# The last inverse products of a long convolution, split by token tile and moved around its frequency loop

## The chip, the cores and the metric

The kernel runs on one core of one Trainium2 chip. The metric is the device time of one execution in microseconds: before the change the median of three runs is 718.02 us (716.53 to 719.85). All matmuls work on fp32 data, or on fp32 data split into a high and a low part.

## The reference, cut to what matters

One adaLN block over 2048 tokens of 512 channels: a diagonal state-space convolution, added to the input, then a Dense-Mish-Dense MLP with 1792 hidden units, added again.

```python
mod = (silu(c) @ w_mod)                 # six rows of 512: sa, ca, ga, sb, cb, gb
h = layernorm(x) * (1 + ca) + sa
K = einsum("dn,dnl,dn->dl", C, exp(dt*A*l), dt*B).real     # the convolution's kernel
y = irfft(rfft(h padded) * rfft(K padded))[:2048] + h * Dskip
x = x + ga * y
h = layernorm(x) * (1 + cb) + sb
x = x + gb * (mish(h @ w1 + b1) @ w2)
```

## The kernel before, in words

The FFT is a matrix product in two stages, on both sides. The kernel has four parts in time.

**Generation** (to about 247 us). 32 groups of 16 channels go through `s_ang`, `s_sin`, `comb`, `s_kgen`, `s_ks`, `s_skip`, `s_ka` and `s_tm`; the last two apply the first DFT stage to K, and `s_tm` copies each group into its columns of the SBUF tile `gk` (128 x 32 x 512). In the same loop the tokens get their first layer norm and their first DFT stage (`pua`) and go out to the DRAM tensor `ud`. Which call stands in which of the 32 turns is a table (`pe`, `se`, `ve`, `vt`, filled by `at`). The six vectors of the modulation come from `mod_mm` (the first three) and, near the end of the loop, `mod_piece` (tile `pmq`).

**The frequency loop** (to 343.5 us), 16 steps q. A step has three products of four matmuls each: `pub` (second DFT stage of the tokens, from `ur`, which is loaded from `ud`), `pkb` (second stage of K, from `gk`), and `pz`, the first inverse stage of the step before. Between them VectorE makes the complex product Y of `pub` (copied to `f` by ScalarE) and `pkb`: two multiplications of 128x1024 and two sums of 128x512. `pz` has 128 output rows for each of the two frequencies of q; ScalarE copies it to `z`, which goes to the DRAM tensor `zd`. In the loop w1 is loaded too, in eight pieces (`w1s`), each split by a cast on ScalarE (`w1h`) and a subtraction on VectorE (`w1l`).

**Between the loop and the MLP.** Rows 32t to 32t+31 of every `pz` belong to token tile t (512 tokens). `z_load` reads a tile's rows back in another order (`zl`), `inv_a` applies the second inverse stage (`pia`), adds the result to x and takes the statistics, `ln_norm` normalizes (`xn`), and `ln_t` transposes (`pln`), applies the modulation on VectorE (`hf`) and on ScalarE (`hh`, the high part), and subtracts the two for the low part.

**The MLP**, four token tiles of 14 hidden blocks: `mm1` (`pm`, 12 matmuls), Mish on ScalarE, a split into `mah` and `mal`, and, two blocks later (LAG), `mm2` (`po`, 12 matmuls). The later tiles do their `z_load`, `inv_a`, `ln_norm` and `ln_t` inside the tile before. `load_w2` loads w2 in four pieces during the first blocks and splits them (`w2h`, `w2l`).

**What sets the order.** Every instruction goes through helpers, so that nearly all of them have one line in the profile (L147 the matmuls, L119 VectorE and ScalarE); names of tiles tell them apart. Matmuls issued by `mm` keep the order of the program; those of the MLP, issued directly, are ordered by the framework's scheduler. VectorE and ScalarE keep the order of the program where the flags `V.on`, `A.on` are set, which is so only in the generation. Each DMA is issued by the instruction stream of the engine that is named: `nc.sync` is SyncE, which does nothing else; a DMA issued through `A` takes its turn on ScalarE. Tile pools opened on the place of closed ones wait for the users of the old tiles.

Of the kernel before, what the change touches and what calls it, by code (L numbers as in the profile page):

```python
# [36 lines left out]
def _constants():  # L37
# [25 lines left out]
    for d in range(16):  # L63
# [21 lines left out]
def s4_block(ctx, tc, io, out):  # L85
# [532 lines left out]
    for n, k, d in ((0, 4, ve), (1, 7, vt), (2, 10, ve), (3, 12, ve), (4, 15, vt), (5, 17, ve), (6, 20, ve), (7, 23, vt)):  # L618
# [13 lines left out]
    at(se, NG - 1, mod_last)  # L632
    at(se, NG - 6, second_part)
    at(se, NG - 2, ur_load, 0)
    at(se, NG - 1, ur_load, 1)
    at(pe, NG - 1, pub, 0, psum)
    at(se, NG, pub_out, 0)

    for k in range(NG + 1):
        tc.cur_priority = 100000 + 10000 * k  # L640
        for s in [(s_kgen, k - 1), (s_ang, k + 3), (s_ka, k - 3)] + pe.get(k, []):
# [19 lines left out]
    s_skip(NG - 1)  # L661
    for f in s_ka, s_tm:
        f(NG - 2)
    for f in s_ka, s_tm:
        f(NG - 1)
    pub(1, psum)
    pub_out(1)
    V.on = A.on = False
# [42 lines left out]

    def inverse(q):
        p = pair("pz", f"pz{q}", 1)
        mi = MQ["mi", q // 4].rearrange("p (q c) x -> p q c x", c=2)
        for c in range(2):
            for r in range(2):
                mm(p[:, r, :], mi[64 * r:64 * r + 64, q % 4, c, :], Y[q][64 * r:64 * r + 64, c, :],
                         start=(c == 0), stop=(c == 1))
        z = yp.tile([P, 2, D], F32, tag="z", name=f"z{q}")
        A.copy(z, p)  # L720
        nc.sync.dma_start(view(zd, 2 * q * D, [[ZROW, P], [1, 2 * D]]), z.rearrange("p r d -> p (r d)"))

# [29 lines left out]
    def z_load(tt, hv):  # L752
        z = ZL[tt, hv] = mp.tile([P, 2, 2, D], F32, tag="z", name=f"zl{tt}{hv}")
        for g in range(4):
            (A if tt == 0 and g % 2 else nc.sync).dma_start(z[32 * g:32 * g + 32].rearrange("p j t d -> p (j t) d"),
                              view(zd, (8 * (4 * tt + g) + 4 * hv) * ZROW, [[D, 32], [ZROW, 4], [1, D]]))

    def inv_a(tt, hv):
        for j in range(2 * hv, 2 * hv + 2):
            p = bank("pia")  # L760
            for tl in range(2):
                T.matmul(p[64 * tl:64 * tl + 64, :], di, ZL[tt, hv][:, j % 2, tl, :], start=True, stop=True)  # L762
            x = X2[tt][:, j]
            V.tensor_add(x, x, p)
            st = keep.tile([P, 6], F32, tag="bst2", name="bst2", bufs=2)
            V.bn_stats(st, x)
            V.bn_aggr(mv2[:, 4 * tt + j, :], st)
# [22 lines left out]
    def mm1(tt, f):  # L790
# [4 lines left out]
        for k in range(KB):  # L795
            for wi, hi in ((0, 0), (0, 1), (1, 0)):
                T.matmul(p, w1[wi][:, k, fs], hh[:, hi, k, :], start=(n == 0), stop=(n == 3 * KB - 1))  # L797
# [9 lines left out]
    def mm2(tt, f, qs=range(4)):  # L807
# [3 lines left out]
        for q in qs:  # L811
            n = 0
            for ai, wi in ((0, 0), (0, 1), (1, 0)):
                T.matmul(PO[tt][q], a[ai][:, P * q:P * q + P], w2[wi][:, f, :],  # L814
                         start=(f == 0 and n == 0), stop=(f == FB - 1 and n == 2))
# [10 lines left out]
    V.tensor_scalar(modt[:, 1], modt[:, 1], 1.0, None, op0=OP.add)  # L826
# [19 lines left out]
    for n, (tt, f) in enumerate(seq):  # L846
        mm1(tt, f)
        if n < 4:
            load_w2(4 * n)
        if tt + 1 < 4:  # L850
            if f == 4:
# [56 lines left out]
```

## Time and profile before

| | us |
|---|---|
| median of three runs | 718.02 |
| the profiled execution, its own time | 714.55 |
| its span, first to last instruction | 712.8 |
| TensorE busy in the span | 634.3 (89%) |
| VectorE busy | 412.8 (58%) |
| ScalarE busy | 319.9 (45%) |

The profile is of one execution. Times in its rows count from the start of the span. A row of the timeline has start, duration, engine, line, operation, output and inputs, and in brackets the idle time of the engine just before and what ended it; a row of the chain of waits has start and duration of a piece of the chain that ended last. PE is TensorE, DVE is VectorE, ACT is ScalarE; SPq and ACTq are the DMA issues of SyncE and ScalarE. PEclk is the TensorE clock that was granted, as a share of full speed.

### The profile page before, as it was taken

Reading aid. Unit: us, or ns where it says so; the run is one execution under the profiler, and the core shown is the slowest. Engines: PE = TensorE matmul, PEld = TensorE weight load, DVE = VectorE, ACT = ScalarE, POOL = GpSimd, SP = SyncE. Lnnn points to the kernel's source line nnn. Section 1 sums busy time; section 2 is a strip of 40 time slices with the busy share of each in tenths; the row PEclk is TensorE's granted clock in tenths of the full one; section 3 lists DMA queues with packets and bytes.
Section 4 is the critical chain, followed back from the end, with each engine's and each line's share of the span. In section 5 each row is a group of like instructions: output and inputs, shape, how many; then the busy total and the mean of one; then the engine's idle time right before and its main releaser. Section 6 shows DMA issues by size and latency. Waiting matters only on the chain.

```text
span 712.8 us, 11831 instructions
## 1 busy us (share of the span) xinstructions
PE 634.3 (89%) x4848; PEld 432.8 (61%) x4848; DVE 412.8 (58%) x813; ACT 319.9 (45%) x466; POOL 5.0 (1%) x12
## 2 busy tenths in 40 slices
PE   0488899889989979999249999999999999999995
PEld 0356666556656623333028778887788867888884
DVE  8889989997976657876196242342443224441113
ACT  2477798598897644543135212322132211322220
POOL 2000000000000000000000000000000000000000
PEclk9969979879969999999669999999999999999999
DMA  7842213624342479973686140052201400020002
GB/s 194 296 135 66 90 41 111 195 74 151 118 146 93 133 202 316 307 228 131 163 240 139 37 101 0 1 119 59 60 1 29 90 0 1 1 57 4 0 1 59
DMA packets 34315, 74.63 MB, mean 105 GB/s; under 512 B 5419, under 2 KB 9903, under 8 KB 33749
## 3 DMA queue, kind: packets, MB, share of 16 engines
q1 hardware_dynamic: 33380, 72.17, 34.9%
q10 hardware_dynamic: 576, 1.05, 0.7%
q8 instruction: 38, 0.62, 0.4%
q0 software_dynamic: 304, 0.66, 0.4%
q14 instruction: 17, 0.13, 0.1%
HBM read 49.73 MB, written 24.13 MB: 104 GB/s over the span
## 4 chain that ended last, share of the span: by engine, by line
PE 69%; DVE 21%; ACT 4%; DMA 3%; issue 2%; SPq 0%; ACTq 0%; DVEq 0%
PE pm L797 22%; PE po L814 22%; DVE ec L119 8%; PE pub L147 4%; PE pz L147 4%; DVE raw L119 4%; PE pkb L147 4%; PE pang L147 3%; PE pkg L147 2%; PE pka L147 2%; PE pia L762 2%; PE pco L147 2%; DVE x L119 1%; PE pua L147 1%; ACT ec L141 1%
## 5 line engine op out<-in xcount | busy, mean ns | idle before, releaser
L797 PE MATMUL pm<-hh,w1h 128*128 128x512 f32 x448 | 142.5, 398 | 0.6 <-ACT hh L119 0.6
L141 ACT ACTIVATE mh<-pm,b 128x512 f32<-128x512 f32 x56 | 38.5, 688 | 228.2 <-PE pm L797 228.2
L119 DVE TENSOR_TENSOR mal<-mh,mah 128x512 fp32r<-128x512 f32 x56 | 38.7, 691 | 155.3 <-ACT mah L119 155.0
L797 PEld LDWEIGHTS pm<-hh,w1h 128*128 128x128 f32 x448 | 84.8, 189 | 21.6 <-ACT hh L119 1.5
L814 PE MATMUL po<-w2h,mah 128*128 128x512 f32 x224 | 89.4, 399 | 0.0
L797 PE MATMUL pm<-hh,w1l 128*128 128x512 f32 x224 | 88.7, 396 | 0.0
L814 PE MATMUL po<-w2l,mah 128*128 128x512 f32 x224 | 88.6, 395 | 0.0
L814 PE MATMUL po<-w2h,mal 128*128 128x512 f32 x224 | 88.5, 395 | 0.0
L119 DVE TENSOR_TENSOR ec<-ec,co 128x1024 f32<-128x1024 f32 x64 | 75.0, 1204 | 8.4 <-ACT ec L141 8.4
L147 PE MATMUL pang<-ac,s 96*128 96x512 f32 x128 | 53.2, 461 | 25.8 <-DMA s<-pkd 25.8
L147 PEld LDWEIGHTS pkg<-ec 128*32 128x32 f32 x2048 | 35.9, 114 | 29.4 <-issue 15.4
L119 DVE TENSOR_TENSOR y<-pkb,f 128x1024 f32<-128x1024 f32 x32 | 37.7, 1220 | 27.5 <-PE pkb L147 27.5
L814 PEld LDWEIGHTS po<-w2h,mah 128*128 128x128 f32 x224 | 42.1, 188 | 14.6 <-ACT mah L119 4.9
L147 PE MATMUL pkg<-ec 128*32 128x64 f32 x2048 | 42.0, 230 | 7.6 <-DVE ec L119 6.7
L797 PEld LDWEIGHTS pm<-hh,w1l 128*128 128x128 f32 x224 | 42.3, 189 | 10.0
L814 PEld LDWEIGHTS po<-w2h,mal 128*128 128x128 f32 x224 | 42.1, 188 | 10.2
L814 PEld LDWEIGHTS po<-w2l,mah 128*128 128x128 f32 x224 | 42.1, 188 | 9.8
L147 PEld LDWEIGHTS pang<-ac,s 96*128 96x128 f32 x128 | 27.6, 215 | 32.9 <-issue 26.3
L147 PE MATMUL pang<-am,s 96*128 96x512 f32 x128 | 43.5, 425 | 0.0
L147 PE MATMUL pco<-mc,s 64*128 64x512 f32 x64 | 30.4, 624 | 11.2 <-ACT co L141 7.1
L141 ACT ACTIVATE ec<-ec,halfpi 128x1024 f32<-128x1024 f32 x32 | 37.5, 1173 | 0.0
L147 PE MATMUL pka<-bdk,ks 128*64 128x128 f32 x512 | 36.5, 288 | 0.9 <-ACT gk L119 0.9
(97 smaller groups left out, 832.2 us busy)
## 6 DMA issues: line engine op xcount, KB each, us to landing
ud<-u SPq DMA_DIRECT2D x16, 512.0 KB, 3.4
ur<-ud SPq DMA_DIRECT2D x32, 256.0 KB, 4.3
zd<-z SPq DMA_DIRECT2D x16, 512.0 KB, 3.3
zl<-zd SPq DMA_DIRECT2D x28, 256.0 KB, 4.9
x<-in_A_u SPq DMA_DIRECT2D x32, 128.0 KB, 3.0
x<-in_A_u SPq DMA_DIRECT2D x8, 512.0 KB, 6.9
out<-ot SPq DMA_DIRECT2D x32, 128.0 KB, 2.3
w1s<-in_B_w SPq DMA_DIRECT2D x8, 448.0 KB, 6.0
```

The costliest lines, as they stand in the source:

```text
L119: ins = getattr(self.engine, name)(*a, **kw)
L141: follow("act", nc.scalar.activation(out, in_, f, **kw))
L147: follow("pe", T.matmul(out, lhsT, rhs, start=start, stop=stop))
L762: T.matmul(p[64 * tl:64 * tl + 64, :], di, ZL[tt, hv][:, j % 2, tl, :], start=True, stop=True)
L797: T.matmul(p, w1[wi][:, k, fs], hh[:, hi, k, :], start=(n == 0), stop=(n == 3 * KB - 1))
L814: T.matmul(PO[tt][q], a[ai][:, P * q:P * q + P], w2[wi][:, f, :], start=(f == 0 and n == 0), stop=(f == FB - 1 and n == 2))
```

## The change

1. **Steps 8 to 15 split the inverse product.** New functions `first` and `first_out` compute only the 32 output rows of token tile 0, with 32 weight columns a matmul; the four steps of a group go to four column groups of the array, so that one tile `pf` holds four steps. Steps 8 to 11 are done at step 12, steps 12 to 15 at step 15. The full `inverse` of steps 8 and 9 runs at steps 14 and 15; those of steps 10 to 15 (`late`) run after the loop, three before `pia` and three behind it. They compute all 128 rows, and store rows 32 to 127.
2. **The rows of tile 0 have their own DRAM tensors** (`z0d`), and are loaded by `zl_load` in three groups into `gk`; the first two inside the loop. The layout of `di` has a second copy for that order of rows. In steps 0 to 7 `inverse` stores `z` in three DMAs in place of one, and all of these DMAs are issued by ScalarE.
3. **Y overwrites K** in `gk` (`product`), which frees the tiles `y1` and, once `pz` is done, the place for item 2.
4. **`pub` runs two steps ahead** of `pkb`, and `pz` stands behind both; `pub` of step 1 moves into the generation, with the loads of `ur`, `w_mod` and the second pair of DFT matrices moved earlier.
5. **The modulation row is loaded as 8 x 128** (`modr`) and transposed on TensorE, in place of a load of single elements.
6. **Program order** now binds the matmuls of the MLP, too, and VectorE and ScalarE from the end of the loop until the fifth block of the MLP.
7. **The last tile's results** use four buffers in place of two, and half of their stores go through ScalarE's queue.

```diff
+    z0d = {(g, r): dram.tile([32 * n, D], F32, name=f"z0d{g}{r}") for g, n in enumerate((8, 4, 4)) for r in range(2)}
...
-    for k, pieces in (20, range(4)), (22, (4, 5)), (23, (6, 7)), (26, (8, 9)), (29, (10, 11)):
+    for k, pieces in (20, range(4)), (20, (4, 5)), (23, (6, 7)), (25, (8,)), (25, (9,)), (27, (10,)), (27, (11,)):
...
-        at(pe, NG - 5 + k, mod_piece, k)
+        at(pe if k else vt, 26 + k, mod_piece, k)
...
-    at(pe, NG - 1, pub, 0, psum)
-    at(se, NG, pub_out, 0)
+    at(se, 30, load_mq, 1)
+    for q in range(2):
+        at(pe, 29 + q, pub, q, psum)
+        at(se, 30 + q, pub_out, q)
...
     def product(q):
-        if q > 1:
-            ur_load(q)
-            pub(q, psum)
-            pub_out(q)
...
-        y = Y[q] = yp.tile([P, 2, D], F32, tag="y1", name=f"y1_{q}")
+        y = Y[q] = gk[0][:, 2 * q:2 * q + 2, :]
...
-    def inverse(q):
-        p = pair("pz", f"pz{q}", 1)
+    def inverse(q, p, pool, tag):
...
-        nc.sync.dma_start(view(zd, 2 * q * D, [[ZROW, P], [1, 2 * D]]), z.rearrange("p r d -> p (r d)"))
+        if q < 8:
+            for r in range(2):
+                A.dma_start(z0d[0, r][32 * q:32 * q + 32], z[0:32, r])
+        A.dma_start(view(zd, 32 * ZROW + 2 * q * D, [[ZROW, 96], [1, 2 * D]]), z[32:P].rearrange("p r d -> p (r d)"))
+
+    def first(g, qs):
+        if g not in PF:
+            PF[g] = pair("pz", f"pf{g}", 1)
+        for c in range(2):
+            for r in range(2):
+                for q in qs:
+                    mm(PF[g][32 * (q % 4):32 * (q % 4) + 32, r, :], mi(q, c, r, slice(0, 32)),
+                       Y[q][64 * r:64 * r + 64, c, :], start=(c == 0), stop=(c == 1))
+
+    def first_out(g):
+        for r, (copy, queue) in enumerate(((V.tensor_copy, nc.sync), (A.copy, A))):
+            z = yp.tile([P, D], F32, tag="z", name=f"zf{g}{r}")
+            copy(z, PF[g][:, r, :])
+            queue.dma_start(z0d[g - 1, r], z)
...
+    def zl_load(g, r):
+        q, n = ((0, 8), (8, 4), (12, 4))[g]
+        k = 64 * r + 4 * q
+        nc.sync.dma_start(gk[0][k:k + 4 * n, 0:8, :], view(z0d[g, r], 0, [[8 * D, 4 * n], [D, 8], [1, D]]))
+
+    for q in range(NQ):
+        product(q)
...
+        if q + 2 < NQ:
+            pub(q + 2, psum)
+            pub_out(q + 2)
+        if 0 < q <= 8:
+            inverse(q - 1, pair("pz", f"pz{q - 1}", 1).rearrange("p r d -> r p d"), yp, "z")
+        if q in (10, 11):
+            zl_load(0, q - 10)
+        if q == 12:
+            first(2, range(8, 12))
+            first_out(2)
+        if q >= 14:
+            inverse(q - 6, pair("pa", f"pz{q - 6}", 1).rearrange("p r d -> r p d"), io4, "i")
...
+        if q == 15:
+            first(3, range(12, 15))
+            first(3, (15,))
+            first_out(3)
+            for r in range(2):
+                zl_load(2, r)
...
-                T.matmul(p, w1[wi][:, k, fs], hh[:, hi, k, :], start=(n == 0), stop=(n == 3 * KB - 1))
+                mm(p, w1[wi][:, k, fs], hh[:, hi, k, :], start=(n == 0), stop=(n == 3 * KB - 1))
...
-            nc.sync.dma_start(rows(out, tl, 4 * tt + q, 1), o[64 * tl:64 * tl + 64])
+            (A if tt == 3 and tl else nc.sync).dma_start(rows(out, tl, 4 * tt + q, 1), o[64 * tl:64 * tl + 64])
...
+    V.on = A.on = True
+    for q in range(10, 13):
+        late(q)
     for hv in range(2):
-        z_load(0, hv)
-    for hv in range(2):
-        inv_a(0, hv)
-        ln_norm(0, 2 * hv, 2)
+        run(inv_a(0, hv))
+    for q in range(13, 16):
+        late(q)
...
+    for ops in ln_norm(0, 0, 4):
+        run(ops)
     ln_t(0)
```

**TensorE from the last steps of the loop to the first block of the MLP.** A row has line, operation, output, inputs, size and, with x, how many follow one another. Before:

```order
L147 MATMUL pub_3506<-ur_3503,mf_3279 64x512 x4
L147 MATMUL pkb_3513<-gk,mf_3279 64x512 x4
L147 MATMUL pz_3524<-y_14_3489,mi_3281 128x512 x4
L147 MATMUL pz_3536<-y_15_3518,mi_3281 128x512 x4
L762 MATMUL pia<-zl_3559,di 64x512 x4
L762 MATMUL pia<-zl_3564,di 64x512 x4
```

Now:

```order
L150 MATMUL pub_3440<-ur_3412,mf_3350 64x512 x4
L150 MATMUL pf_3447<-gk,mi_3216 32x512 x16
L150 MATMUL pkb_3471<-gk,mf_3350 64x512 x4
L150 MATMUL pub_3481<-ur_3437,mf_3350 64x512 x4
L150 MATMUL pkb_3488<-gk,mf_3350 64x512 x4
L150 MATMUL pz_3498<-gk,mi_3216 128x512 x4
L150 MATMUL pkb_3510<-gk,mf_3350 64x512 x4
L150 MATMUL pz_3520<-gk,mi_3216 128x512 x4
L150 MATMUL pf_3528<-gk,mi_3352 32x512 x16
L895 MATMUL pmt<-ident,modr 128x8
L150 MATMUL pz_3572<-gk,mi_3216 128x512
L150 MATMUL pia<-gk,di 64x512 x8
```

Steps 9 to 13 have no `pz` any more; two groups of 16 short matmuls stand in the loop. Behind the second come the three late inverses of four matmuls each (the row of `pz_3572` is the first of the twelve), then `pia`, then the other three.

**ScalarE at the start of the loop.** Before:

```order
L144 ACT_TABLE_LOAD
L119 CAST w1h<-w1s_3085 128x896
L119 CAST w1h<-w1s_3147 128x896
L119 COPY z_3082<-pz_3077 128x1024
L119 COPY f_3097<-pub_3092 128x1024
L119 COPY z_3115<-pz_3110 128x1024
```

Now:

```order
L147 ACT_TABLE_LOAD
L122 CAST w1h<-w1s_3116 128x896
L122 CAST w1h<-w1s_3180 128x896
L122 COPY f_3084<-pub_3079 128x1024
L122 COPY f_3104<-pub_3099 128x1024
L122 COPY z_3111<-pz_3106 128x1024
L122 DMA z0d_79<-z_3111 32x512
L122 DMA z0d_80<-z_3111 32x512
L122 DMA zd<-z_3111 96x1024
L122 CAST w1h<-w1s_3248 128x896
L122 COPY f_3138<-pub_3133 128x1024
```

Three DMA issues follow each copy `z`. The copies `f` of steps 2 and 3 come before the first `z`, both behind the two first casts, as `z` of step 0 was.

**VectorE, the modulation of token tile 0** (`hh0`; the numbers tell the four pieces apart). Before:

```order
L119 TENSOR_SCALAR hf_3639<-pln_3634,modt_3044 128x512
L119 TENSOR_SCALAR hf_3648<-pln_3643,modt_3044 128x512
L119 TENSOR_TENSOR w2l_3674<-w2s4_3723,w2h_3673 128x512
L119 TENSOR_TENSOR hh0_3633<-hf_3639,hh0_3633 128x512
L119 TENSOR_TENSOR hh0_3633<-hf_3648,hh0_3633 128x512
L119 TENSOR_SCALAR hf_3657<-pln_3652,modt_3044 128x512
L119 TENSOR_SCALAR hf_3666<-pln_3661,modt_3044 128x512
```

Now:

```order
L122 TENSOR_SCALAR hf_3694<-pln_3689,modt_3059 128x512
L122 TENSOR_TENSOR hh0_3688<-hf_3694,hh0_3688 128x512
L122 TENSOR_SCALAR hf_3703<-pln_3698,modt_3059 128x512
L122 TENSOR_TENSOR hh0_3688<-hf_3703,hh0_3688 128x512
L122 TENSOR_SCALAR hf_3712<-pln_3707,modt_3059 128x512
L122 TENSOR_TENSOR hh0_3688<-hf_3712,hh0_3688 128x512
```

The order is now `hf`, low part, `hf`, low part; the splits of w2 stand behind all four pieces.

More of the change, by code (lines that the diff above doesn't have):

```diff
@@ L208, in s4_block @@
     da = conv.tile([P, P], F32, name="da")
-    di = keep.tile([P, 64], F32, name="di")
+    di = keep.tile([P, 2, 64], F32, name="di")
     ident = keep.tile([P, P], F32, name="ident")
@@ L660, in s4_block @@
             step(s_mag, k + 1)
[L661 to L667, printed above, removed]
+    for i in NG - 2, NG - 1:
+        step(s_skip, i)
+        s_ka(i)
+        s_tm(i)
     V.on = A.on = False
@@ L754, in z_load @@
         for g in range(4):
-            (A if tt == 0 and g % 2 else nc.sync).dma_start(z[32 * g:32 * g + 32].rearrange("p j t d -> p (j t) d"),
+            nc.sync.dma_start(z[32 * g:32 * g + 32].rearrange("p j t d -> p (j t) d"),
                               view(zd, (8 * (4 * tt + g) + 4 * hv) * ZROW, [[D, 32], [ZROW, 4], [1, D]]))
     def inv_a(tt, hv):
-        for j in range(2 * hv, 2 * hv + 2):
+        zl = ZL[tt, hv] if tt else gk[0][:, 4 * hv:4 * hv + 4, :].rearrange("p (j t) d -> p j t d", j=2)
+        v = Later()
+        js = range(2 * hv, 2 * hv + 2)
+        for j in js:
             p = bank("pia")
             for tl in range(2):
[L762 to L767, printed above, removed]
+                mm(p[64 * tl:64 * tl + 64, :], di[:, 0 if tt else 1, :], zl[:, j % 2, tl, :])
+            v.tensor_add(X2[tt][:, j], X2[tt][:, j], p)
+        st = [keep.tile([P, 6], F32, tag="bst2", name="bst2", bufs=2) for j in js]
+        for t, j in zip(st, js):
+            v.bn_stats(t, X2[tt][:, j])
+        for t, j in zip(st, js):
+            v.bn_aggr(mv2[:, 4 * tt + j, :], t)
+        return v.ops
     def ln_norm(tt, q0, n):
         i = 4 * tt + q0
-        rsqrt(rst2[:, i:i + n], mv2[:, i:i + n, 1], n, keep, f"rsq{n}")
+        v, w = Later(), Later()
+        rsqrt(rst2[:, i:i + n], mv2[:, i:i + n, 1], n, keep, f"rsq{n}", v)
         for q in range(q0, q0 + n):
             i = 4 * tt + q
-            y = LNX[tt, q] = mp.tile([P, D], F32, tag="xn", name=f"xn{tt}{q}", bufs=4)
-            V.tensor_scalar(y, X2[tt][:, q], mv2[:, i, 0:1], rst2[:, i:i + 1], op0=OP.subtract, op1=OP.mult)
+            y = LNX[tt, q] = mn.tile([P, D], F32, tag="xn", name=f"xn{tt}{q}", bufs=4)
+            w.tensor_scalar(y, X2[tt][:, q], mv2[:, i, 0:1], rst2[:, i:i + 1], op0=OP.subtract, op1=OP.mult)
+        return v.ops, w.ops
     def ln_t(tt):
-        hh = HT[tt] = mp.tile([P, 2, KB, 512], F32R, tag="hh", name=f"hh{tt}")
+        hh = HT[tt] = (mp if tt % 2 else mn).tile([P, 2, KB, 512], F32R, tag="hh", name=f"hh{tt}", bufs=1)
         for b in range(NB):
@@ L813, in mm2 @@
             for ai, wi in ((0, 0), (0, 1), (1, 0)):
-                T.matmul(PO[tt][q], a[ai][:, P * q:P * q + P], w2[wi][:, f, :],
-                         start=(f == 0 and n == 0), stop=(f == FB - 1 and n == 2))
+                mm(PO[tt][q], a[ai][:, P * q:P * q + P], w2[wi][:, f, :],
+                   start=(f == 0 and n == 0), stop=(f == FB - 1 and n == 2))
                 n += 1
@@ L819, in fin_q @@
         x = X2[tt][:, q]
-        o = mp.tile([P, D], F32, tag="ot", name="ot")
+        o = mn.tile([P, D], F32, tag="xn", name="ot", bufs=4) if tt == 3 else mp.tile([P, D], F32, tag="ot", name="ot")
         V.tensor_mul(o, PO[tt][q], gbb)
@@ L823, in fin_q, with late @@
         for tl in range(2):
-            nc.sync.dma_start(rows(out, tl, 4 * tt + q, 1), o[64 * tl:64 * tl + 64])
-    V.tensor_scalar(modt[:, 1], modt[:, 1], 1.0, None, op0=OP.add)
+            (A if tt == 3 and tl else nc.sync).dma_start(rows(out, tl, 4 * tt + q, 1), o[64 * tl:64 * tl + 64])
+    def late(q):
+        inverse(q, [psum.tile([P, 512], F32, tag="po", name=f"pz{q}{r}") for r in range(2)], io4, "i")
+    p = bank("pmt")
+    follow("pe", T.transpose(p[:, 0:8], modr, ident[0:8, 0:8]))
+    V.tensor_copy(modt[:, 0], p[:, 0:4])
+    V.tensor_scalar(modt[:, 1], p[:, 4:8], 1.0, None, op0=OP.add)
     tables("mish")
+    V.on = A.on = True
+    for q in range(10, 13):
+        late(q)
     for hv in range(2):
-        z_load(0, hv)
-    for hv in range(2):
-        inv_a(0, hv)
-        ln_norm(0, 2 * hv, 2)
+        run(inv_a(0, hv))
+    for q in range(13, 16):
+        late(q)
+    left2.close()
+    left.close()
+    mp = ctx.enter_context(tc.tile_pool(name="mp", bufs=2, side="right"))
+    for ops in ln_norm(0, 0, 4):
+        run(ops)
     ln_t(0)
@@ L849, in s4_block @@
             load_w2(4 * n)
+        if n == 4:
+            V.on = A.on = False
         if tt + 1 < 4:
@@ L855, in s4_block @@
             if f in (6, 8):
-                inv_a(tt + 1, f // 2 - 3)
+                run(inv_a(tt + 1, f // 2 - 3))
             if f == 9:
-                ln_norm(tt + 1, 0, 4)
+                for ops in ln_norm(tt + 1, 0, 4):
+                    run(ops)
             if f == 12:
```

76 lines of the change are left out of this document (46 added, 30 removed).

## The prediction

> **What bounds the kernel now.** I read the busy time by stage first, then the chain of waits, then single rows. In the view by stage the columns are the stretch, its length, the busy time of TensorE, its weight loads, VectorE, ScalarE and GpSimd, each with its count of instructions, then the granted clock, the DMA engines' share and GB/s.
>
> ```profile
> 262.00:341.50 79.50, 78.13 (x338) 24.64 (x336) 58.61 (x67) 34.71 (x35) 0.00 (x0) 0.99 0.72 231
> 341.50:357.00 15.50, 4.21 (x14) 1.62 (x16) 0.66 (x2) 1.01 (x1) 0.00 (x0) 0.63 0.76 197
> 357.00:373.00 16.00, 6.73 (x28) 2.86 (x24) 15.24 (x48) 5.05 (x9) 0.00 (x0) 0.71 0.83 242
> 400.00:700.00 300.00, 300.00 (x1310) 235.32 (x1309) 95.83 (x183) 75.94 (x114) 0.00 (x0) 1.00 0.15 32
> ```
>
> TensorE sets the pace of the frequency loop and of the MLP. Between them, for 31.5 us, it is busy for 11. So the MLP can only start earlier, and the loop only lose products. The chain of waits shows the loop's step and what stands between:
>
> ```profile
> 329.12 1.87 PE pub L147 x8
> 330.99 1.72 PE pkb L147 x8
> 332.71 1.92 PE pz L147 x8
> ...
> 341.55 2.00 PE pz L147 x8
> 344.66 2.59 DMA zd<-z
> 347.89 6.44 DMA zl<-zd
> 354.77 1.99 PE pia L762 x4
> 373.14 10.26 PE pm L797 x36
> 383.40 2.79 PE po L814 x12
> ```
>
> A step is 1.87 + 1.72 + 1.92 = 5.5 us. The last product ends at 343.54; the copy, the store to `zd` and the load of `zl` take until 354.77; statistics, norm and transposes until 373.14; and three blocks of `pm` end at 383.40, from where `po` and `pm` alternate without a gap. I compare both kernels at that point, the end of the third `pm`: 383.40 - 343.54 = 39.9 us behind the loop.
>
> **The sum**, against the profiled execution's own 714.55 us (span 712.8; the median of the runs is 3.5 above, and I add the same).
>
> *Into the loop.*
>
> ```profile
> 240.46 1.09 PE L147 MATMUL pka<-bdk,ks 128*64 128x128 f32 x16 [0.85 <-ACT gk L119]
> 250.37 0.58 ACT L119 COPY gk<-pka 128x512 f32<-128x512 f32 x1 [0.49 <-PE pka L147]
> 253.19 3.65 PE L147 MATMUL pkb<-gk,mf 128*64 128x512 f32 x16 [1.16 <-ACT f L119]
> 257.80 0.94 ACT L119 CAST w1h<-w1s 128x896 fp32r<-128x896 f32 x1 [2.41 <-DMA w1s<-in_B_w]
> 259.47 3.02 PE L147 MATMUL pz<-y,mi 64*128 64x512 f32 x8 [2.62 <-DVE y L119]
> 262.42 2.55 PE L147 MATMUL pub<-ur,mf 128*64 128x512 f32 x8
> ```
>
> With two `pub` among the last turns of the generation, the waits of 0.85 and 1.16 go, and one of about 0.6 (the last copy to `gk`, 0.58) comes: 1.4 gained, `pkb` of step 0 at 251.8. Before, 2.62 us passed without a matmul until Y was ready, and the next two groups ran long (3.02 - 1.92 and 2.55 - 1.87, 1.8 together): 4.4. Now two `pub` stand there. But the second needs the tile that ScalarE's copy `f` frees, and that copy is queued behind the two casts, which end at 258.74 with the load; so that `pub` starts at about 259.2, 2 us after `pkb` of step 1 has ended (251.8 + 1.72 + 1.87 + 1.72 = 257.1). I keep 2.4 of the 4.4; the bounds are 0 and 4.4. Sum: 3.8.
>
> *The loop.* Six `pz` leave it: 6 x 1.92 = 11.5. Two groups `pf` come. No row shows 64 rows by 32 columns; the nearest are these:
>
> ```profile
> 241.48 1.06 PE L147 MATMUL pmq<-wm,sc 128*32 128x512 f32 x6
> 332.82 2.36 DVE L119 TENSOR_TENSOR y<-pkb,f 128x1024 f32<-128x1024 f32 x2 [1.82 <-PE pkb L147]
> 335.21 1.30 DVE L119 TENSOR_TENSOR y<-y,y 128x512 f32<-128x512 f32 x2
> ```
>
> `pz` runs its four matmuls two at a time (two row groups) in 1.92, so 0.96 a round; `pmq` runs three in three column groups in 1.06. A `pf` is 16 matmuls on eight different tiles: two rounds, 1.9, if row and column groups add up; four rounds, 3.8, if four run at once. I take 2.0, since `pmq` shows that column groups with different data run together and `pz` the same of row groups. The two cost 4; the bounds are 3.8 and 7.7. In steps 9 to 13 `pkb` and `pub` are 3.6 us, and VectorE's part of a step 3.7 (332.82 to 336.51): there it sets the pace, but over the whole tail TensorE's sum (30.1 us from `pkb` 9 to the end of `pf`) still covers it. The wait for the last Y stays, now ahead of `pf` of step 15. So 11.5 - 4 = 7.5.
>
> [...]
>
> Against it stands ScalarE, which now issues the stores:
>
> ```profile
> 334.71 1.02 ACT L119 COPY z<-pz 128x1024 f32<-128x1024 f32 x1 [2.62 <-PE pz L147]
> 347.50 1.80 ACTq L119 DMA_DIRECT2D zl<-zd  x4
> ```
>
> An issue takes 0.45 us. In the first steps ScalarE has `f` and `z` (1.0 each), three issues (1.35) and a cast or two (0.94 each): 4.3 to 5.3 of 5.5 us, and what waits for a load there (the 2.41 above) now holds the copies and the stores behind it. From below the cost is 0, from above the 2.41 three times, 7.2: I take 2. Loop: 5.5 gained; together with the entry the last `pf` ends at 343.5 - 9.3 = 334.2.
>
> *From the loop to the MLP.* All loads of `zl`, from issue to landing:
>
> ```profile
> DMA to landing us min/median/max: 3.3/5.0/9.9
> ```
>
> A copy of 0.6 to 0.7, a store (2.59 before, for twice the bytes: 2.4), and a load of twice 256 KB in place of 2 MB (the shortest landing, 3.3, plus 0.9 for two issues): 7.4 us to `pia` in place of 11.2. Three late inverses, 5.8 us, fit in, and three more behind `pia`, where VectorE is the chain:
>
> ```profile
> 356.86 0.69 DVE L119 TENSOR_TENSOR x<-x,pia 128x512 f32<-128x512 f32 x1 [14.85 <-PE pia L762]
> 358.31 0.18 DVE L119 BATCH_NORM_AGGREGATE mv<-bst 128x2 f32<-128x6 f32 x1
> 360.16 0.17 DVE L119 TENSOR_SCALAR rsq<-mv 128x2 f32<-128x2 f32 x1
> 361.75 0.16 DVE L119 SCALAR_TENSOR_TENSOR rst<-rsq,rst 128x2 f32<-128x2 f32 x1
> 364.55 0.99 DVE L119 TENSOR_SCALAR xn<-x,mv,rst 128x512 f32<-128x512 f32 x2
> 371.47 1.53 DVE L119 TENSOR_SCALAR hf<-pln,modt 128x512 f32<-128x512 f32 x2
> ```
>
> The first two `pia` 0.95, four sums and four statistics of 0.69, four aggregates of 0.18: 7.2; twelve small operations at 0.2 (nine lie between 360.16 and 361.91), 2.4 where there were 24 (two roots become one); four `xn`, 2.0; transposes and semaphores 0.5. That is 12.1 us from `pia` to the first `hf`, against 371.47 - 354.77 = 16.7.
>
> Then the new order costs. ScalarE's `hh` waits for `hf`, and the low part for `hh`:
>
> ```profile
> 448.66 0.81 DVE L119 TENSOR_SCALAR hf<-pln,modt 128x512 f32<-128x512 f32 x1
> 449.51 0.78 ACT L119 ACTIVATE hh<-pln,modt 128x512 fp32r<-128x512 f32 x1 [0.74 <-DVE hf L119]
> 450.32 0.69 DVE L119 TENSOR_TENSOR hh<-hf,hh 128x512 fp32r<-128x512 f32 x1 [0.25 <-ACT hh L119]
> ```
>
> With `hf` of one piece behind the low part of the piece before, a piece takes 0.85 + 0.81 + 0.69 = 2.35 us, four 9.4, and the first block, bound to its place, ends 0.5 later; two more blocks are 5.6: 15.5, where it was 383.40 - 371.47 = 11.9. Since the first block keeps TensorE busy for a third of that time, the clock counts:
>
> ```profile
> 256.90:259.40 2.50, 0.00 (x0) 0.00 (x0) 2.50 (x4) 0.94 (x1) 0.00 (x0) 1.00 1.08 249
> 259.40:262.40 3.00, 2.93 (x8) 0.83 (x8) 3.00 (x5) 0.00 (x0) 0.00 (x0) 0.65 0.84 186
> 374.00:376.40 2.40, 2.40 (x6) 1.91 (x7) 2.40 (x5) 1.91 (x4) 0.00 (x0) 0.51 0.41 85
> ```
>
> A pause of 2.5 us is followed by 3 us at 0.65; from the first `pm` at 373.14 half the clock lasts to 376.4 at least, 3.3 us. The same here costs half of that, 1.5. Behind the loop: 7.4 + 12.1 + 15.5 + 1.5 = 36.5, against 39.9: 3.4 gained. [...]
>
> w2 is loaded when the last late store has landed:
>
> ```profile
> 358.49 0.40 SPq L840 DMA_DIRECT2D w2s<-in_B_w  x1
> 364.43 2.18 ACT L119 CAST w2h<-w2s 128x512 fp32r<-128x512 f32 x4 [19.80 <-DMA w2s<-in_B_w]
> ```
>
> The last late copy ends some 18.5 us behind `pf`, its store 21, the load (5.9) 27; its casts are due after the first Mish at 31: covered, by 4 us. The 1024-element load of `modt` was off the path, so item 5 is worth nothing.
>
> *The end.*
>
> ```profile
> 705.92 0.69 DVE L119 TENSOR_TENSOR ot<-po,gbb 128x512 f32<-128x512 f32 x1 [1.64 <-DMA out<-ot]
> ```
>
> Four buffers take that wait away: 1.6.
>
> Total: 3.8 + 5.5 + 3.4 + 1.6 = 14.3. Profile 714.55 - 14.3 = 700.2; median 718.0 - 14.3 = **703.7 us**.
>
> **The rivals.**
> *Faster still*: no wait for casts or stores (2), `pub` at the entry not held (2), the clock kept (1.5): 20, so 698. For it, the rows of 262 to 341 show no stall with casts in line; against it, the stores leave SyncE, which had nothing else.
> *ScalarE as the bound of the first steps*: each cast waits for a load, the load for a buffer, and the stores stand behind. Price: the 7.2 above in place of 2, and once the 1.8 of slowed groups that followed a pause before: 7.0, so 711. For it, the DMA share in the entry's rows is 1.08 and 0.84, so that loads that come earlier land later; against it, `f` is now needed two steps after it is made.
> *w2 late*: its load landed after 5.9 us before; the longest `zl` took 9.9, and the last late store could be slower by as much. With 8 us in all, 4 beyond the cover are lost: 708. With 15, 715: no measurable change.
> *Slower*: the `pf` matmuls run one after another, 16 x 0.96 = 15.4 each. Then the two cost 31 in place of 4, and the time is 703.7 + 27 = 731; it decides from 2.0 + 14.3/2 = 9.2 us a group on. Against it: three `pmq` in 1.06.
>
> **Chances.** The forecast (700 to 707) 0.50, faster still 0.22, ScalarE 0.17, w2 late 0.07 (a third of it within the noise), slower 0.04. What a measurement can tell from no change is about 0.5%, 3.6 us: so faster 0.91 (the upper end of ScalarE's case falls within), same 0.05, slower 0.04. Range 694 to 712, with the first three cases in it; the forecast's own is 700 to 707.
>
> **What would show it.** `pf` groups of about 2 us; `pkb` of step 0 at 251.8; steps 2 to 8 at 5.5 us, and where longer, `pub` or `pz` waiting for ScalarE; the last `pf` ending near 334 and `pia` 7.4 behind; four pieces of `hf` 2.35 apart; the third `pm` done 36.5 behind `pf`; TensorE without a gap from there. The forecast is wrong if `pf` takes over 4 us, if the loop's steps grow, or if `po` waits for `w2h`.

## The result, and the profile after

The changed kernel takes **713.0 us** (median of 7, 710.1 to 714.9) where the kernel before takes 717.8 (median of 7, 716.5 to 719.9): a ratio of 0.9932, 95% interval 0.9913 to 0.995, so it is 0.7% or 4.8 us faster. Forecast were 703.7 us, in a range of 694 to 712. The direction is right, the gain a third of the forecast, and the time lies 1 us above the range.

The profiled execution of the changed kernel took 713.02 us (span 711.2). That of before took 714.55, 3.2 less than its median, so the two traces differ by 1.5 us only. They are compared by the lengths of the stages, each between two rows that both traces have: the first `pkb`; the end of the last `pz` (before) or `pf` (after); the first `hf` of the first token tile; the first `po`; the start of the last `pm`; the end of the last `ot`.

| stage, us | before | forecast | after |
|---|---|---|---|
| start of the first `pkb` | 253.2 | 251.8 | 252.8 |
| loop: to the end of the last `pz` or `pf` | 90.4 | 82.4 | 89.1 |
| to the first `hf` | 27.9 | 19.5 | 20.7 |
| to the first `po` | 11.8 | 17.0 | 17.5 |
| to the last `pm` | 313.6 | 313.6 | 317.2 |
| to the end of the last `ot` | 11.9 | 10.3 | 10.3 |

(Forecast column: 334.2 - 251.8; 7.4 + 12.1; 15.5 + 1.5; no gap; 11.9 - 1.6.) Two stages are off: the loop by 6.7 us and the MLP by 3.6. The one behind the loop came nearly as worked out, its loss at `hf` included.

**The loop.** The view by stage, first after, then before (stretch, length, busy time of TensorE, its weight loads, VectorE, ScalarE and GpSimd with their counts, granted clock, DMA share, GB/s):

```profile
262.00:282.00 20.00, 19.62 (x86) 5.91 (x82) 14.85 (x18) 8.42 (x10) 0.00 (x0) 1.00 0.97 293
282.00:302.00 20.00, 15.63 (x61) 4.73 (x63) 13.96 (x15) 8.53 (x10) 0.00 (x0) 0.91 0.84 256
```

```profile
282.00:302.00 20.00, 20.00 (x88) 6.27 (x86) 15.94 (x18) 9.82 (x11) 0.00 (x0) 1.00 1.00 318
```

In 282 to 302 TensorE, busy throughout before, stood still for 4.4 us and lost more to the clock (granted 0.91). The timeline of TensorE of the changed kernel shows where (in brackets the idle time and what ended it):

```profile
279.68 1.94 PE L150 MATMUL pkb<-gk,mf 128*64 128x512 f32 x8
282.88 1.94 PE L150 MATMUL pub<-ur,mf 128*64 128x512 f32 x8 [1.26 <-ACT f L122]
285.79 1.99 PE L150 MATMUL pz<-gk,mi 64*128 64x512 f32 x8 [0.97 <-ACT z L122]
287.70 1.94 PE L150 MATMUL pkb<-gk,mf 128*64 128x512 f32 x8
...
293.88 3.18 PE L150 MATMUL pz<-gk,mi 64*128 64x512 f32 x8 [2.52 <-ACT z L122]
296.99 2.39 PE L150 MATMUL pkb<-gk,mf 128*64 128x512 f32 x8
...
323.55 1.94 PE L150 MATMUL pub<-ur,mf 128*64 128x512 f32 x8 [2.29 <-DMA ur<-ud]
325.42 1.95 PE L150 MATMUL pf<-gk,mi 64*32 64x512 f32 x32
...
338.57 3.31 PE L150 MATMUL pf<-gk,mi 64*32 64x512 f32 x32
...
351.14 3.65 PE L150 MATMUL pia<-gk,di 128*64 128x512 f32 x16 [2.28 <-DMA zd<-z]
...
366.49 0.50 PE L150 MATMUL pm<-hh,w1h 128*128 128x512 f32 x1 [0.80 <-ACT hh L122]
...
467.31 0.50 PE L150 MATMUL po<-w2h,mah 128*128 128x512 f32 x1 [0.78 <-DVE ot L122]
```

`pkb` starts 8.0 us apart, then 9.3, where 5.5 were forecast; the waits are for ScalarE's copies `f` and `z`, and after the longest the next two groups run at a lower clock (3.18 us for 1.99, granted 0.61 from 293.8 to 297.1; then 2.39 for 1.94, granted 0.80 from 297.0 to 299.4). ScalarE's timeline of that stretch:

```profile
280.98 0.94 ACT L122 CAST w1h<-w1s 128x896 fp32r<-128x896 f32 x1 [4.46 <-DMA w1s<-in_B_w]
281.82 1.01 ACT L122 COPY f<-pub 128x1024 f32<-128x1024 f32 x1
283.89 0.94 ACT L122 CAST w1h<-w1s 128x896 fp32r<-128x896 f32 x1 [1.05 <-DMA w1s<-in_B_w]
284.73 1.00 ACT L122 COPY z<-pz 128x1024 f32<-128x1024 f32 x1
...
289.99 0.94 ACT L122 CAST w1h<-w1s 128x896 fp32r<-128x896 f32 x1 [0.67 <-DMA w1s<-in_B_w]
291.98 0.94 ACT L122 CAST w1h<-w1s 128x896 fp32r<-128x896 f32 x1 [1.05 <-DMA w1s<-in_B_w]
292.82 1.01 ACT L122 COPY z<-pz 128x1024 f32<-128x1024 f32 x1
```

Each copy that TensorE waits for follows, without a pause, a cast of w1 that waited for its load. Later `pub` of step 14 waits 2.29 us for `ur`. The `pf` cost what was forecast, 1.95 (the second group's 3.31 holds the wait for the last Y).

**The MLP.** Totals of waits in the changed kernel (time, times, longest); the first line belongs to the loop:

```profile
ACT w1h L122 <- DMA w1s<-in_B_w: 13.8, 8, 4.5
...
PE po L150 <- DVE ot L122: 2.3, 3, 0.8
```

TensorE waits once at each border between token tiles, for the fourth `po` of a new tile (467.31 above). VectorE's timeline there, and ahead of it that of the first tile's modulation:

```profile
362.55 0.81 DVE L122 TENSOR_SCALAR hf<-pln,modt 128x512 f32<-128x512 f32 x1 [0.42 <-PE pln L847]
364.21 0.69 DVE L122 TENSOR_TENSOR hh<-hf,hh 128x512 fp32r<-128x512 f32 x1 [0.84 <-ACT hh L122]
364.82 0.80 DVE L122 TENSOR_SCALAR hf<-pln,modt 128x512 f32<-128x512 f32 x1
...
464.63 0.69 DVE L122 TENSOR_TENSOR ot<-po,gbb 128x512 f32<-128x512 f32 x1 [1.77 <-DMA out<-ot]
465.36 0.70 DVE L122 TENSOR_TENSOR ot<-ot,x 128x512 f32<-128x512 f32 x1
465.97 0.69 DVE L122 TENSOR_TENSOR mal<-mh,mah 128x512 fp32r<-128x512 f32 x1
466.57 0.68 DVE L122 TENSOR_TENSOR ot<-po,gbb 128x512 f32<-128x512 f32 x1
```

The third `ot` waits 1.77 us for a buffer, so the fourth (466.57) empties the last `po` bank of the old tile late, and the new tile's fourth `po` stands, now in written order, ahead of the next `pm`. Before, matmuls of the next `pm` stood there, the last of that `po` behind them:

```profile
469.70 0.40 PE L797 MATMUL pm<-hh,w1h 128*128 128x512 f32 x1
...
470.86 0.40 PE L814 MATMUL po<-w2h,mah 128*128 128x512 f32 x1
```

A piece of `hf` takes 2.27 us (362.55 to 364.82), as forecast (2.35).

### The profile page after: what moved, and what is told of

It reads as the page before. It is cut to its first block, busy times and chain, and to the rows that moved or that the text cites. A ratio compares the mean times of both kernels' runs of the same rounds, so it can differ in the third digit from the quotient of the medians.

```text
span 711.2 us, 11977 instructions
## 1 busy us (share of the span) xinstructions
PE 640.9 (90%) x4913; PEld 434.2 (61%) x4913; DVE 412.8 (58%) x804; ACT 321.1 (45%) x474; POOL 5.0 (1%) x12
## 4 chain that ended last, share of the span: by engine, by line
PE 62%; DVE 22%; DMA 8%; ACT 4%; issue 2%; SPq 1%; DVEq 0%; ACTq 0%
PE pm L150 21%; PE po L150 20%; DVE ec L122 6%; DVE raw L122 4%; PE pang L150 4%; DMA w1s<-in_B_w 3%; PE pkg L150 3%; PE pka L150 3%; DVE ot L122 2%; PE pia L150 2%; PE pz L150 2%; PE pco L150 2%; PE pua L150 1%; DVE x L122 1%; PE pub L150 1%
## 5 line engine op out<-in xcount | busy, mean ns | idle before, releaser
L150 PE MATMUL pm<-hh,w1h 128*128 128x512 f32 x448 | 144.3, 402 | 3.1 <-ACT hh L122 2.4
L122 ACT CAST mah<-mh 128x512 fp32r<-128x512 f32 x56 | 34.7, 620 | 1.8
```

What stands on the lines that cost most here:

```text
L122: ins = getattr(self.engine, name)(*a, **kw)
L150: follow("pe", T.matmul(out, lhsT, rhs, start=start, stop=stop))
```

## The experiments

All are edits of the changed kernel, and each ratio is to the kernel before on the same chip; the changed kernel's own is 0.9932. Single executions scatter by several us: in these traces the first `pkb` starts anywhere from 251.4 (e1) to 256.1 us (e5), though no edit touches the generation. So each stage is read from its own start. The length of a stage is still that of one execution, while the ratio is of medians. The lengths, with those of before and after again (e2 is told below):

| us | ratio | loop | to `hf` | to `po` | to last `pm` |
|---|---|---|---|---|---|
| before | 1 | 90.4 | 27.9 | 11.8 | 313.6 |
| changed | 0.9932 | 89.1 | 20.7 | 17.5 | 317.2 |
| e1 casts in place | 0.9954 | 88.2 | 20.4 | 16.4 | 317.2 |
| e3 loads of z behind | 0.9932 | 85.9 | 21.3 | 16.9 | 317.1 |
| e4 MLP unbound | 0.9888 | 89.5 | 21.7 | 16.7 | 314.0 |
| e5 low part a step later | 0.9883 | 79.9 | 21.9 | 17.9 | 317.3 |
| e6 `hf` and MLP unbound | 0.9794 | 89.3 | 21.3 | 10.7 | 314.0 |
| e7 split undone | 1.0077 | 93.6 | 23.1 | 17.5 | 317.1 |
| e8 e3 + e5 + e6 | 0.9746 | 80.8 | 20.7 | 10.7 | 314.0 |
| e9 e5 + e6 | 0.9710 | 81.8 | 20.7 | 10.7 | 314.2 |

**e1: ScalarE and VectorE in written order in the loop.** My theory: the casts of w1 hold the copies. The rival: the stores that ScalarE now issues do.

```
+    V.on = A.on = True
     for q in range(NQ):
```

> Changed against the changed kernel: in the frequency loop ScalarE and VectorE keep the written order, so that each cast of w1 and its low part stand behind the copies f and z and the stores of their step, where they stood up to four steps ahead. Casts theory (a cast that waits for its load holds the copies f and z behind it; measured waits 1.74 at the entry, then 3.45, 4.46, 1.05, 0.67 and 1.05): steps 5 to 7 fall from 8.0 and 9.3 to about 5.5 each, the last pf ends 5 to 8 us earlier (334 to 337 in place of 341.9), and the kernel takes 705 to 708 us, 0.982 to 0.986 of before. Stores theory (three issues of 1.35 us a step on ScalarE, and their transfers, hold the loop, whatever the place of the casts): the last pf stays within 2 us of 341.9, 711 to 713 us.

Measured: 713.5 us (12 executions), 0.9954 (0.9935 to 0.9973); the loop took 88.2. No cast waits for its load any more, but the waits stay. The totals of waits of VectorE (250 to 320), then of TensorE (250 to 312):

```profile
DVE w1l L122 <- ACT w1h L122: 18.0, 6, 3.7
```

```profile
PE pub L150 <- ACT f L122: 6.2, 6, 2.0
```

In written order the low part `w1l`, which needs the cast, stands ahead of the next step's Y on VectorE. The cast now stands behind `z` and three issues on ScalarE, so VectorE waits 18 us for casts, Y comes late, the buffer of `f` with it, and `pub` waits as before. The time is about the rival's (711 to 713), its cause isn't shown: one queue was mended and the other held. e5 mends both.

**e2: the stores of steps 0 to 7 issued by SyncE**, the casts where the changed kernel has them.

```
-                A.dma_start(z0d[0, r][32 * q:32 * q + 32], z[0:32, r])
-        A.dma_start(view(zd, 32 * ZROW + ...
+                nc.sync.dma_start(z0d[0, r][32 * q:32 * q + 32], z[0:32, r])
+        (nc.sync if q < 8 else A).dma_start(view(zd, 32 * ZROW + ...
+    A.on = True        # and load_w1 called where the changed order has its casts
```

> Changed: the stores of z of steps 0 to 7 are issued by SyncE in place of ScalarE; all else on ScalarE keeps the order of the changed kernel, the early casts too. Stores theory: the waits of pub and pz for ScalarE in steps 5 to 7 (1.26, 0.97, 2.52) go, the last pf ends 4 to 7 us earlier, 706 to 709 us. Casts theory: the casts still wait for their loads (3.5 and 4.5), and since SyncE's loads now stand behind stores that wait for z, some come later still: the last pf ends between 1 us earlier and 6 later than 341.9, 712 to 719 us.

Measured: 716.9 us, 1.0003 (0.9986 to 1.002), with a loop of 88.6. The casts still wait for their loads, 10.8 us in all (13.8 in the changed kernel), and hold `z`; ScalarE, then TensorE:

```profile
290.17 0.94 ACT L122 CAST w1h<-w1s 128x896 fp32r<-128x896 f32 x1 [1.41 <-DMA w1s<-in_B_w]
```

```profile
292.07 1.99 PE L150 MATMUL pz<-gk,mi 64*128 64x512 f32 x8 [3.26 <-ACT z L122]
```

The time is what the casts theory said (712 to 719). Taking the stores from ScalarE doesn't shorten the loop. This alone doesn't clear the stores: in SyncE's queue they wait for `z`, with loads behind them, and `pub` has two new waits, 0.83 and 2.70 us, whose end the profile doesn't name. e5, where ScalarE still issues the stores, decides. Why the kernel is even slower than the changed one its profiled execution (712.70 us) doesn't show; that stays open.

**e5: as e1, with the low part behind the next step's Y.**

```
         A.copy(w1[0][:, k, cs], t)
-        V.tensor_sub(w1[1][:, k, cs], t, w1[0][:, k, cs])
+        LOW.append(lambda: V.tensor_sub(w1[1][:, k, cs], t, w1[0][:, k, cs]))
...
+    V.on = A.on = True
     for q in range(NQ):
...
         product(q)
+        while LOW:
+            LOW.pop(0)()
```

> Changed: as e1 (ScalarE and VectorE in written order in the loop, each cast of w1 behind the copies and stores of its step), but the low part of w1 stands behind the next step's four operations of y on VectorE, so that y no longer waits for a cast. Casts theory: with the casts' waits for loads gone (e1 showed none) and VectorE not held, steps 2 to 8 take 5.5 us each, no pub or pz waits over 0.3 us for ScalarE there, and from the first pkb to the end of the last pf 82 to 85 us pass in place of 89.1 (e1: 88.2); 707 to 709 us, 0.986 to 0.988 of before. Rival, the DMA engines set the pace (share 0.9 to 1.03 between 262 and 292): something else waits for loads (pub for ur, pkb for mf), 87 to 89 us, 711 to 713 us.

Measured: 707.4 us, 0.9883 (0.9856 to 0.991), with a loop of **79.9** us in place of 89.1. The view by stage and TensorE's timeline:

```profile
282.00:302.00 20.00, 20.00 (x90) 6.28 (x88) 15.70 (x18) 9.90 (x11) 0.00 (x0) 1.00 0.98 302
```

```profile
287.49 1.94 PE L150 MATMUL pkb<-gk,mf 128*64 128x512 f32 x8
289.26 1.89 PE L150 MATMUL pub<-ur,mf 128*64 128x512 f32 x8
291.07 1.99 PE L150 MATMUL pz<-gk,mi 64*128 64x512 f32 x8
292.99 1.94 PE L150 MATMUL pkb<-gk,mf 128*64 128x512 f32 x8
```

TensorE has no gap where the changed kernel loses 4.4 us, with the DMA engines at a share of 0.98. So neither their rate nor the stores, which ScalarE still issues, set the loop: the place of eight casts and eight low parts in two queues did. e1 and e5 differ by the place of the low parts alone, and their loops by 8.4 us.

How much this is worth is less sure than that it is the cause. The loop of this trace is 9.2 us shorter than the changed kernel's, but it began 3.3 us later (256.1), which may favour it: its `pub` never waits for `ur`, while that of the changed kernel waits 2.29 us. Behind it 1.7 us are lost again in `pia`, where the clock is lower than in the changed kernel (0.83 from 342 to 352, there 1.00; last section). In e8 and e9, which keep these two orders and began 1.9 and 1.5 us later, the loop takes 80.8 and 81.8 us, 8.3 and 7.3 shorter. By the ratios the edit is worth less: 3.5 us here (0.9932 to 0.9883; 1 to 6 with both intervals), and 6.0 from e6 to e9 (0.9794 to 0.9710; 3 to 9). What the medians lose against the traces stays open.

**e3: the loads into gk's place behind the loads of `ur`.**

```
-        if q in (10, 11):
-            zl_load(0, q - 10)
+        if q == 13:
+            for r in range(2):
+                zl_load(0, r)
```

> Changed: the two loads of the first eight rows' z into gk's place are issued in step 13 in place of steps 10 and 11, so that the loads of ur of steps 14 and 15 are ahead of them in SyncE's queue. If they held these loads (queue theory), the wait of pub of step 14 or 15 for ur (2.29 us) goes, the last pf ends about 2 us earlier (340), and pia, which needs pf's own rows last, starts as far behind it as now (9.2): 711 us, 0.990. Rival, the pause is VectorE's anyway (its part of a step, 3.7 us, sets the pace in steps 9 to 15): the pub wait goes, pkb or pf waits for f or y instead, no gain, 713. Loss, if the loads into gk's place then land behind pf's rows: pia later by 1 to 3 us, 714.

Measured: 711.5 us, 0.9932 (0.9912 to 0.9952). In the trace the wait of 2.29 is gone and the loop is 3.2 us shorter, but the ratio is that of the changed kernel. **e9** asks again, beside e8:

> Changed: as e8, but the two loads of the first eight rows' z stand in steps 10 and 11 again, as in the changed kernel. If the queue theory of e3 holds (its loop was 2 us shorter in the profile, its time no better), this is 2 us above e8: 699 to 700 us, 0.977, with pub of step 13 or 14 waiting about 2 us for ur. If the place of these loads is worth nothing, as e3's time and e5's trace say (0.96 for ScalarE there, none for ur): 696 to 698 us, 0.973 to 0.976.

Measured: 696.8 us, 0.9710 (0.9686 to 0.9734), against 0.9746 (0.9718 to 0.9774) for e8. In both the `pub` made for step 14 waits for `ur`; e8, then e9:

```profile
317.27 1.94 PE L151 MATMUL pub<-ur,mf 128*64 128x512 f32 x8 [1.96 <-DMA ur<-ud]
```

```profile
317.81 1.94 PE L151 MATMUL pub<-ur,mf 128*64 128x512 f32 x8 [2.87 <-DMA ur<-ud]
```

With the loads moved the wait is 0.9 us shorter and the kernel no faster. The place of these loads isn't the cause of the wait. e5 has e9's loop, and there `pub` waits 0.96 us for `f` and not for `ur`, so the wait differs from execution to execution; what makes `ur` late stays open.

**e4: TensorE unbound from the fifth block of the MLP on.**

```
-        follow("pe", T.matmul(out, lhsT, rhs, start=start, stop=stop))
+        ins = T.matmul(out, lhsT, rhs, start=start, stop=stop)
+        if bound[0]:
+            follow("pe", ins)
...
-            V.on = A.on = False
+            V.on = A.on = bound[0] = False
```

> Changed: from the fifth block of the MLP on TensorE's instructions are no longer bound to the written order; what moves is one group of three po, the last quarter of a tile's first po, behind the next block of pm at each of the three borders between token tiles (and a few pia). Order theory (TensorE waits there 0.8 us each, 2.3 together, for VectorE to empty the bank of po): from the end of the third pm to the last pm 313.8 to 314.9 in place of 317.4, 709.5 to 711 us, 0.989. Rival: the 2.3 us come from somewhere else (the buffer of ot, which waits 1.77 for the store of the output), and the gap only moves to the next po: 313.8 isn't reached, 712.5 to 713.5.

Measured: 707.3 us, 0.9888 (0.9858 to 0.9919). Its profiled execution was a long one, 713.84 us, whose loop began 3.2 us later than the changed kernel's (256.03). Its MLP has no wait; e4, then the changed kernel:

```profile
390.00:690.00 300.00, 300.00 (x1308) 235.02 (x1308) 97.34 (x186) 76.82 (x116) 0.00 (x0) 1.00 0.18 39
```

```profile
390.00:690.00 300.00, 297.71 (x1295) 232.30 (x1295) 94.72 (x182) 74.58 (x112) 0.00 (x0) 1.00 0.17 37
```

Three matmuls moved behind a `pm`, three times, give back 3.1 of the 3.6 us lost in the MLP (317.17 - 314.04); by the ratios it is 3.2. From 384 to 700 us TensorE has no wait left, so no gap moved to the next `po`, and the rival falls.

**e6: unbound from the first tile's modulation on** (e4 is in it).

```
+    V.on = A.on = bound[0] = False
     ln_t(0)
```

> Changed: the written order ends before the first tile's modulation instead of after four blocks of the MLP: hf of a second piece stands ahead of the low part of the first, on TensorE the first two blocks of pm are interleaved, and e4's change at the tile borders is in it. Serial theory (hf, hh and the low part one after the other, 2.26 us a piece, with TensorE mostly idle so that it then runs at half the clock): from the first hf to the end of the third pm 12 to 14 us in place of 17.5, then 314 as in e4; 703 to 705.5 us, 0.982 to 0.985. Rival: the clock falls there whatever the order, and the chain of VectorE (8 operations of 0.7 to 0.8 us) is the bound: 16 to 17, and the time is e4's, 706 to 708 us.

Measured: 702.2 us, 0.9794 (0.9757 to 0.983). From the first `hf` to the first `po` 10.7 us pass, less than before the change (11.8). VectorE's timeline, then the view by stage, and that of the changed kernel for the same two pieces of work:

```profile
364.47 1.53 DVE L123 TENSOR_SCALAR hf<-pln,modt 128x512 f32<-128x512 f32 x2 [0.42 <-PE pln L850]
366.13 1.41 DVE L123 TENSOR_TENSOR hh<-hf,hh 128x512 fp32r<-128x512 f32 x2
367.46 1.52 DVE L123 TENSOR_SCALAR hf<-pln,modt 128x512 f32<-128x512 f32 x2
369.11 1.41 DVE L123 TENSOR_TENSOR hh<-hf,hh 128x512 fp32r<-128x512 f32 x2
```

```profile
364.40:368.20 3.80, 3.17 (x20) 2.40 (x19) 3.57 (x6) 1.50 (x2) 0.00 (x0) 1.00 0.38 116
368.20:375.10 6.90, 6.90 (x31) 5.56 (x30) 4.23 (x8) 4.83 (x8) 0.00 (x0) 1.00 0.91 309
```

```profile
362.50:369.30 6.80, 4.29 (x20) 2.24 (x17) 4.21 (x6) 2.33 (x3) 0.00 (x0) 1.00 0.63 194
369.30:376.20 6.90, 6.30 (x14) 4.18 (x15) 3.38 (x7) 3.96 (x7) 0.00 (x0) 0.52 1.07 295
```

With two pieces ahead VectorE never waits for `hh`, and with two blocks of `pm` interleaved TensorE is busy 3.17 of the first 3.8 us (4.29 of 6.8 in the changed kernel) and keeps the full clock, where the changed kernel falls to 0.52 for 6.9 us. Both halves of the loss, the chain and the clock, come from the written order. Against e4 the stage is 6.0 us shorter, and the ratios give 6.7.

**e7: the split alone undone.** All sixteen inverses whole in the loop, no `pf`, no late ones; the rest of the change stays.

```
-        if 0 < q <= 8:
+        if 0 < q:
             inverse(q - 1, ...
-        if q == 12:
-            first(2, range(8, 12))
-            first_out(2)
...
-    for q in range(10, 13):
-        late(q)
```

> Undone: the split alone. All sixteen inverses stand whole in the loop, one a step, the last behind the last product, and store the first tile's rows into the same tensors; no pf, no late inverses; everything else of the change stays. If TensorE's time in the loop is worth what its sum says (six pz of 1.92 less two pf of 1.95), the last inverse ends 7 to 8 us later than the last pf did (349), and the kernel takes 719 to 721 us, 1.003 to 1.006 of before. Rival, that VectorE (3.7 us a step) and the loads cover part of it: 2 to 5 us, 714 to 718 us, 0.997 to 1.001.

Measured: 720.6 us, 1.0077 (1.0048 to 1.0105). Against the changed kernel the loop is 4.5 us longer, the way to the first `hf` 2.4. TensorE's row shows the second:

```profile
356.23 5.32 PE L150 MATMUL pia<-gk,di 128*64 128x512 f32 x16 [8.29 <-DMA gk<-z0d]
```

By the traces the split is worth 6.9 us, by the ratios 10 (1.0077 - 0.9932 is 1.45% of 716; some 8 to 13 with both intervals). The time is the first theory's, the length of the loop the rival's (2 to 5 us). And without it the change would have made the kernel slower: the casts, the written order at `hf` and in the MLP cost more than its other parts gain.

**e8: e3, e5 and e6 together.**

> Changed: e3, e5 and e6 (with e4) in one kernel. If the terms add up: 2.2 of the loads behind ur, 4 to 6 of the casts, of which 1 to 2 are lost again because VectorE sets the pace in steps 9 to 15, 3.1 at the tile borders and 3.5 to 5.5 of the first tile's modulation: 11 to 15 us below the changed kernel, 698 to 702 us, 0.974 to 0.980 of before. If they don't add (the loads move the wait elsewhere, the clock falls anyway): 704 to 707 us.

Measured: 697.2 us, 0.9746 (0.9718 to 0.9774). That is 13.3 us below the changed kernel by the ratios, within the 11 to 15 expected. In the trace the loop is 8.3 us shorter than the changed kernel's, `hf` to `po` 6.8, the MLP 3.1: 18.2, of which 1.9 go again because the loop began later. So the stages of one trace add up to more than the medians show. e8 and e9, which differ by nothing that these runs settle, are the fastest kernels of the study, 2.5 to 2.9% below before.

## Why the prediction was wrong, step by step

- **Into the loop (3.8 gained): nearly right.** The first `pkb` came at 252.8, not 251.8. `pub` was forecast for about 259.2 and started at 259.39. Step 2 starts 1.6 us earlier than before with one `pub` (1.87) more behind it, 3.5 together.
- **The loop: the price of ScalarE failed.** The step said: from below 0, from above 7.2, "I take 2". Without that 2 the sum gives a loop of 80.4 us; the three loops with the casts mended take 79.9, 80.8 and 81.8. So the rest of the sum held, and the price in the traces was 7.3 to 9.2 us (89.1 less these), at my upper bound or above it; by the ratios 3.5 and 6.0, which is still more than 2. The mechanism stood among the rivals (ScalarE as the bound of the first steps, 0.17, 711 us), and e1 and e5 settle which part of it: the casts and their low parts, not the stores. The price was too low because it went by one wait, 2.41. Before, five casts waited:

```profile
ACT w1h L119 <- DMA w1s<-in_B_w: 7.7, 5, 2.6
```

After, eight waits add up to 13.8, the longest 4.46, and the clock falls behind the longest of TensorE's own waits (2.52 us, then 0.61 from 293.8 to 297.1). The order was there to be read. The casts' row, before and after (shortest, median and longest in ns, first and last start):

```profile
L119 ACT CAST w1h<-w1s x8: 937/938/942, 254.5 to 301.6; 128x896 fp32r<-128x896 f32 x8
```

```profile
L122 ACT CAST w1h<-w1s x8: 937/938/939, 255.8 to 292.0; 128x896 fp32r<-128x896 f32 x8
```

The same eight casts stand in 36 us instead of 47, in four pairs, and the last of each pair stands right ahead of an `f` or a `z`. A place ahead of a copy is free only while the cast's load has landed.
- **`pf`: right.** 1.95 forecast as 2.0. The slower case (731 us) had hung on this alone.
- **From the loop to `hf`: 1.2 off.** `pia` starts 9.3 us behind `pf`, not 7.4. The chain has a late store, `zd<-z`, just ahead of `pia`; that the last rows share the DMA engines with the late stores is likely, but not tested. From `pia` to the first `hf` 11.4 passed, where 12.1 were forecast.
- **`hf` to `po`: right in sum** (17.5 for 17.0), and by luck in part. The four pieces took 9.1 us (362.55 to 371.67) where 9.4 were forecast, the blocks behind them 8.4 where 6.1 and 1.5 for the clock were: by this difference the clock, 0.52 from 369.3 to 376.2, cost about 2.3, not 1.5. e6 shows that the loss was not needed.
- **The MLP: a term was missing.** "No gap" went unexamined. The edit binds `po` and `pm` of the whole MLP to the written order, and at a border that order puts a `po` whose bank isn't empty ahead of a `pm` that could run: 3.6 us, of which e4 gives back 3.1.
- **w2 and the end: right.** No `po` waits for `w2h`; the tail is 1.6 us shorter.
- **From profile to median: 3.5 us that hid part of the miss.** I added before's distance between trace and median to the forecast. But before's trace was a short execution and the changed kernel's took what its median takes. So the median is 9.3 us above the forecast, while in trace terms the forecast, 700.2, was 12.8 us low: first `pkb` 1.0, loop 6.7, to `hf` 1.2, to `po` 0.5, MLP 3.6, less 0.3 in the last store.

So the 14.3 us were there, and more: e8 and e9 are 13 to 16 us faster than the changed kernel by their ratios, with the split untouched. What hid the gain were three orders of instructions that the same edit brought: the casts in the loop, the pieces of `hf`, the `po` at the borders.

## What to carry to other kernels

When an edit frees the bounding engine, go through the in-order queues that serve it once more. Whatever stands there ahead of a copy it needs, and itself waits for a load, had slack only because the step was longer. A written order that helps in one stretch should end where the stretch ends: bound on into the MLP it cost 3.1 us, and around the modulation 6.8. And price a stall by which instruction stands behind which, not by one wait that the old trace happens to show.

## What the runs showed of the hardware that I had not expected

- The granted clock fell without a long pause. In the changed kernel it is 0.52 from 369.3 to 376.2, after 6.8 us in which TensorE was busy for 4.29 and no wait was above 0.80. In e6, busy 3.17 of 3.8 at the same place, it stayed at 1.00.
- The same pause had two outcomes. Ahead of `pia` TensorE waits 1.9 to 2.4 us in all of these kernels but e7. In the changed kernel, e1, e2, e8 and e9 `pia` then took 3.65 us, in e3, e4, e5 and e6 5.35. The row of e5, to be held against 351.14 above:

```profile
345.06 5.35 PE L150 MATMUL pia<-gk,di 128*64 128x512 f32 x16 [1.97 <-DMA zd<-z]
```

So in these runs the length of the pause doesn't decide it. In e5 the granted clock is 0.83 from 342 to 352, with `pia` at 345.06 to 350.41, and in e6 0.68 from 352.2 to 357.5, the length of its `pia`; in the changed kernel it is 1.00 from 351 to 355. The 1.7 us are part of the column "to `hf`" above, and no edit of the four kernels aims at them. What decides it no run shows.
- A change of tile on the array was hardly dearer than none, 0.10 us between the two rows compared. In the changed kernel 1.71 us pass from the start of a `pub` (128*64 in its row) to that of the next group where it is a `pkb`, 128*64 too (310.22 to 311.93), and 1.81 where it is a `pz`, 64*128 (264.95 to 266.76). The sum has no term for the four changes that `pf` brings. Whether they cost anything these loops can't tell: they lie between 0.5 below and 1.4 above the 80.4 us of the sum.
